# First-stage order of a chunked-attention and two-FFN kernel: products in sub-steps, an early ScalarE table load, and a new table of order

## The chip, the cores and the metric

The kernel runs on one core of one Trainium2 chip. The metric is device time in microseconds (us) of one execution. A core has TensorE (PE in the profile, with PEld for its weight loads), VectorE (DVE), ScalarE (ACT), GpSimd (POOL) and SyncE (SP, which here only starts DMA transfers), each with its own queue of instructions; they meet through semaphores.

## The reference, cut to what matters

```python
# q, k, v: (4, 8, 768, 64); mem_k, mem_v: (4, 8, 8, 64); chunks of 32 queries
for c in range(nc):                       # each chunk sees 8 memory keys + 16 left + 32 own + 8 right
    scores = scale * q_c @ concat(mem_k, k_ctx).T
    a = exp(scores - max(scores)); a = a / (sum(a) + 1e-9)
    out[:, :, c_start:c_end] = a @ concat(mem_v, v_ctx)
x = out.transpose(0, 2, 1, 3).reshape(3072, 512)
h = x @ w_in;  r = max(h, 0);  x = (s * (r * r) + b) @ w_out         # first FFN, 512 -> 2048 -> 512
h = x @ w_in2; x = (max(h, 0) + alpha * min(h, 0)) @ w_out2          # second FFN
```

The four weight matrices arrive as 64-bit floats.

## The kernel before, in words

The 3072 tokens are 24 tiles of 128, and six blocks of four tiles (512 tokens). For each tile the attention makes scores (`sc`), VectorE takes the row maxima (`m`), ScalarE the exponentials (`e`, or `qa` where the tile shares a borrowed buffer), VectorE sums and normalises, TensorE transposes (`pt`, or `turns`), ScalarE copies the result (`aT`), and TensorE multiplies by the values (`px`; `sp` is a bank that takes the scores of one tile and the values of the tile before). Tiles 0 to 3 (`ALONE`) have banks of their own pair; from tile 4 on, one scores-and-values step per tile.

Every factor of a large product is split in a high and a low part of 32 bits, and three products are summed: high by high, high by low, low by high. ScalarE makes the high part of the attention's output (`xh`) and VectorE the low part (`xl`). The weights are handled in 16 parts of 128 hidden columns, `w0` to `w15`, each with an input half and an output half (for `w0` and `w1` the halves, `w0i` and `w0o`, are loaded and converted separately). A conversion takes the raw words through seven passes: ScalarE (`a<-raw`), four on VectorE (L299, L304, L309, L314), ScalarE's high part (L321), VectorE's low part (L327).

A unit is one block and one part f: 12 products into a `ph` bank (function `g1`, L633), an activation in three steps, a split into `gh` and `gl`, and, two units later (`LAG`), 12 products into the four `po` banks (`g2`, L692). The first block's parts 0 to 2 (`HALVES`) are done in two halves of 256 tokens, the left half first. In the first FFN, block 0 goes through its first `SEG` parts, then block 1 through the same ones; both are spilled to DRAM, and each is finished with the remaining parts afterwards. Blocks 2 to 5 then take all 16 parts, and the second FFN follows.

The order of all this is decided when the kernel is built: a class `Plan` holds a list of steps with an engine, a rank and what they wait for, and puts out the steps engine by engine; `Pace` describes TensorE's clock and instruction refills for it. Constants in the class (`RATE`, `FETCH`, and now `AHEAD`) and tables of numbers (`FIRST_LOADS`, the order of the first loads on SyncE's queue; `TILE_RANKS`; `CONV_RANKS`; `STEPS`; `BY_HEAD`, the tiles whose exponentials are taken head by head) set the order in the first stage. What comes out is a fixed sequence for each engine; on the chip each engine runs its own in that order. The ring of `ph` banks has two places, and no more than eight of SyncE's transfers are under way at once.

Of the kernel before, what the change touches and what calls it, by code (L numbers as in the profile page):

```python
# [9 lines left out]
F32 = mybir.dt.float32  # L10
F32R = mybir.dt.float32r
U32 = mybir.dt.uint32
ACTF = mybir.ActivationFunctionType
# [3 lines left out]
P = 128  # L17
# [9 lines left out]
KD, KF = DM // P, DFF // P  # L27
BLK = 512
TPB = BLK // P
# [2 lines left out]
NEG = -1.0e30  # L32
SCALE = 1.0 / float(D) ** 0.5

SEG = 7
LAG = 2
HALVES = 3
PIECES = 2
SPLIT = 2

# [2 lines left out]
SET_SLOTS = {2: 15, 3: 14}  # L43
QA_SLOT = 13

FIRST_LOADS = """q0 q1 w1i v0 q3 w0o q2 v2 w0i v1 w1o q4 v3 w2 w3 w4 v4 w6 q5 v7 q6 v5 q7 w5 w9 v6 w7 w8""".split()

TILE_RANKS = (-280, -85, -170, -175, -15, -240, -5, -260, -85)

BY_HEAD = (1, 2, 4, 5, 6)  # L50

CONV_RANKS = {1: 195, 2: 35, 3: 30, 4: 25, 5: 20, 6: 15, 9: -40, 10: -95, 11: -25, 12: -10, 13: 40, 14: -70}

STEPS = (28, 18, 18, 47, 43, 38)


KHEAD = LEFT + RIGHT
# [25 lines left out]
class Pace:  # L83


    WINDOW, PHASE = 3.41, 2.7
    BLOCK, FIRST = 256, 184

    def __init__(self):
        self.window, self.active, self.warm = 0, 0.0, False  # L90
# [11 lines left out]
    def run(self, t, step, fetch):  # L102

        done, total = 0, max(step.count, 1)
        while done < total:
            at = self.count + done
            block, into = divmod(at - self.FIRST, self.BLOCK)
            if block >= 0 and into == 0:
                t = max(t, self.due[block])
                self.due[block + 1] = t + fetch(t)  # L110
            n = min(total - done, self.BLOCK - into)
            work = step.cost * n / total
            while work > 1e-9:
                self._to(t + 1e-6)
                speed = 1.0 if self.warm else 0.65 if step.dense else 0.53
                left = self.PHASE + (self.window + 1) * self.WINDOW - t
                took = min(left, work / speed)
                self.active += took * (0.5 if step.dense else 1.0)
                work -= took * speed
                t += took  # L120
            done += n
        self.count += total
        return t


class Plan:
# [1 line left out]

    PAST = {"PE": 0.22, "DVE": 0.15, "ACT": 0.2, "POOL": 0.15, "SP": 2.2, "PQ": 2.2}
    NEXT = {"DVE": 0.12, "ACT": 0.12}  # L130
    RATE = 396e3
    LANES = 8
    FETCH = 2.7, 5.3

    def __init__(self, rings):
        self.steps = []
# [10 lines left out]
    def order(self):  # L147
        for s in self.steps:
            s.n_wait = len(s.after)
            for a in s.after:  # L150
                a.outs.append(s)
        engines = {s.engine for s in self.steps}
        open_ = {e: [] for e in engines}
        for s in self.steps:
            if not s.n_wait:
                open_[s.engine].append(s)
        at = {e: 0.0 for e in engines}
        last = {}
        held = {}
        wire = 0.7  # L160
        landed = [0.0] * self.LANES
        pace = Pace()
        due = sorted((s for s in self.steps if s.engine == "SP"), key=lambda s: (-s.rank, -s.seq))
        done = []
        while len(done) < len(self.steps):
            best = None
            for e in engines:
                pick = None
                queue = [due[-1]] if e == "SP" and due else open_[e]
                for s in queue:  # L170
                    if s.n_wait:
                        continue
                    r = s.ready
                    if s.takes:
                        free = self.free[s.takes[0]]
                        if not free:
                            continue
                        r = max(r, min(free.values()))
                    r = max(r, at[e] + (self.NEXT[e] if e in self.NEXT and last.get(e) in s.after else 0.0))
                    if e == "SP" and s.bytes:  # L180
                        r = max(r, landed[-self.LANES])
                    key = (max(r, at[e] + 0.02), s.rank, s.seq)
                    if pick is None or key < pick[0]:
                        pick = (key, r, s)
                if pick and (best is None or pick[1] < best[1]):
                    best = pick
            assert best, [(e, s.rank, s.takes, s.seq) for e in engines for s in open_[e]]
            _, t, s = best
            e = s.engine
            open_[e].remove(s)  # L190
            if e == "SP":
                due.pop()
            slot = None
            if s.takes:
                ring, holder = s.takes
                free = self.free[ring]
                slot = min(free, key=lambda n: (free[n], n))
                del free[slot]
                held[holder] = (ring, slot)
            s.start = t  # L200
            last[e] = s
            at[e] = pace.run(t, s, lambda t: self.FETCH[wire > t + 1.0]) if e == "PE" else t + s.cost
            end = at[e]
            if s.bytes:
                n = max(1, s.bytes >> 18)
                for k in range(n):
                    wire = max(wire, t + s.cost * (k + 1) / n) + s.bytes / n / self.RATE
                    landed.append(wire + self.PAST[e])
                end = wire
            s.end = end + self.PAST[e]  # L210
            for holder in s.frees:
                ring, n = held.pop(holder)
                self.free[ring][n] = s.end
            for o in s.outs:
                o.n_wait -= 1
                o.ready = max(o.ready, at[e] if o.engine == e in ("PE", "DVE", "ACT") else s.end)
                if not o.n_wait:
                    open_[o.engine].append(o)
            done.append((s, slot))
        return done  # L220
# [3 lines left out]
def tile_chunk_attention_two_ffn(ctx: ExitStack, tc: tile.TileContext, qt, kw, vw, win, wout, cst, out):  # L224
    nc = tc.nc
    const = ctx.enter_context(tc.tile_pool(name="const", bufs=1))
# [3 lines left out]
    psum = ctx.enter_context(tc.tile_pool(name="psum", bufs=1, space=bass.MemoryType.PSUM))  # L230
# [4 lines left out]
    xh = [const.tile([P, KD, BLK], F32R, name=f"xh{n}") for n in range(2)]  # L235
    xl = [const.tile([P, KD, BLK], F32R, name=f"xl{n}") for n in range(2)]
# [3 lines left out]
    plan = Plan({"ph": 2, "g": 2, "gg": 3, "ao": 2})  # L240
    slot_of = {}

    def held(holder):
        return slot_of[holder]
# [18 lines left out]


    wts, raws, conv_done, load_done = {}, {}, {}, {}

    def slot_tile(f, mats, shape, dt, name):
        tag = f"w{f}" if len(mats) == 2 else f"w{f}{'io'[mats[0]]}"
# [17 lines left out]
    def convert(layer, f, mats, rank, after):  # L286
        n = len(mats)
# [41 lines left out]
        name = f"w{f}" + ("io"[mats[0]] if n == 1 else "")  # L329
# [7 lines left out]
        hi = plan.add("ACT", 0.02 + 0.51 * n, rank, high, [c4])  # L337
        lo = plan.add("DVE", 0.07 + 0.53 * n, rank, rest, [hi], frees=[key])
        for m in mats:
            conv_done[layer, m, f] = lo  # L340

# [174 lines left out]
    def x_high(i):  # L518
        for pars, px in state[i]["px"]:
            nc.scalar.activation(out=x_of(i, xh, pars), in_=px, func=ACTF.Copy)  # L520
# [35 lines left out]
    def finish_tile(i, r, px):  # L556
        leaves[set_of(i)]["v"] = leaves[set_of(i)]["x"] = px
        more = 0.15 if i in ALONE else 0
        hi = plan.add("ACT", 0.49 + more, r + STEPS[5], lambda: x_high(i), [px] + list(x_users[i // TPB % 2]))
        x_done[i] = plan.add("DVE", 0.61 + more, r + STEPS[5], lambda: x_low(i), [hi])  # L560
        return x_done[i]

# [52 lines left out]
                      [att[t]["aT"] for t in two] + [att[t]["lv"] for t in two], count=256, dense=True)  # L615
        banks_free["pa"] = [finish_tile(t, r3, px) for t in two]

    x_done = {}
    x_users = {0: [], 1: []}


    po = [None] * KD
    ph, gt, gs = {}, {}, {}

    def g1(u):
        layer, j, f, cols = units[u]
        n = (layer * NB + j) % 2
        p = psum.tile([P, BLK], F32, tag=f"ph{held(('ph', u))}", name="ph")[:, :cols.stop - cols.start]
        w = wts[layer, 0, f]
        i = 0  # L630
        for kk in range(KD):
            for a, x in ((1, xh[n]), (0, xl[n]), (0, xh[n])):
                nc.tensor.matmul(p, lhsT=w[:, a, kk * P:(kk + 1) * P], rhs=x[:, kk, cols],  # L633
                                 start=(i == 0), stop=(i == 3 * KD - 1))
                i += 1
        ph[u] = p

    def new_g(u):
        cols = units[u][3]
# [112 lines left out]

    id_ = plan.add("POOL", 0.6, -1000, lambda: make_identity(nc, ident))
    cs = plan.add("ACT", 0.1, -1000, consts)

    for i in range(TPB):
        attention_alone(i, TILE_RANKS[i])
    for i in range(TPB, 2 * TPB + 1):
        r = TILE_RANKS[i]
# [57 lines left out]
    for j in range(2, NB):  # L817
        n_units = (KF - SEG) + 7 if j == 2 else KF
        for i in range(j * TPB, j * TPB + TPB, 2):
            r = when[0, j, 0] - 40 - 10.0 * (TPB - i % TPB) * n_units / TPB  # L820
# [7 lines left out]
    def unit_g1(u):  # L828
        layer, j, f, cols = units[u]
        rank = 10.0 * u  # L830
        n = (layer * NB + j) % 2
        if layer == 0:
            xs = [x_done[j * TPB + t] for t in range(cols.start // P, cols.stop // P)]
        else:
# [3 lines left out]
            xs = [x1_done[j, "x"]]  # L838
        if (layer, j) not in blocks_g1:
# [1 line left out]
            x_users[n] = []  # L841
        width = (cols.stop - cols.start) / BLK
        mm = MM if width == 1 else 0.121
        s = plan.add("PE", 12 * mm, rank, lambda: g1(u), xs + [conv_done[layer, 0, f], id_, in_turn[0]],
                     takes=("ph", ("ph", u)), count=24)
        in_turn[0] = s
        x_users[n].append(s)
        last_user[layer, f, 0] = s
# [156 lines left out]
```

## Time and profile before

| | us |
|---|---|
| median of 3 runs (lowest, highest) | 1143.71 (1139.6, 1144.55) |
| the profiled execution | 1143.53 |
| its span, first to last instruction | 1141.8 |
| TensorE busy | 1114.9 |
| VectorE busy | 605.6 |
| ScalarE busy | 350.8 |
| TensorE busy in the first 60 us | 39.04 |

The span is shorter than the execution by what lies around the instructions. A row of a timeline gives the start, the time busy, the engine, the line, the operation with output and input, the shapes and the count of instructions merged; in brackets stands the idle time before it and what ended it. Products are pipelined, so the time busy of one runs into the next; the distance of two starts is what one costs. The line numbers of the profile before are those of the kernel before; the new kernel's lines lie three to six further on in the parts that are shown.

### The profile page before, as it was taken

What the parts mean: (1) busy time and instruction counts of PE and PEld (TensorE: products, weight loads), DVE (VectorE), ACT (ScalarE), POOL (GpSimd) and SP (SyncE); (2) the same over time, 40 slices, a digit from 0 to 9 for tenths busy, and PEclk for the clock granted to TensorE, in tenths of its full rate; (3) what the DMA queues carried; (4) which work ended last, traced back from release to release, by engine and by line L of the source; (5) the groups of instructions that cost most, each with busy time, mean ns of one, the idle gap of its engine ahead of it and who ended that gap; (6) DMA issues with size and microseconds to landing.
All of it is one profiled execution on the core that took longest, in us unless ns stands there. A gap on an engine that the chain in (4) does not pass through costs nothing.

```text
span 1141.8 us, 18302 instructions
## 1 busy us (share of the span) xinstructions
PE 1114.9 (98%) x7848; PEld 925.2 (81%) x7848; DVE 605.6 (53%) x938; ACT 350.8 (31%) x615; POOL 28.8 (3%) x58
## 2 busy tenths in 40 slices
PE   4799999999999999999999999999999999999998
PEld 4788888888888888888888788888888888888886
DVE  6797935445445355434799744334334434344432
ACT  5675644432232223224564311111111111111111
POOL 0000000000000000000000000000000000000000
PEclk9899999999999999999999999999999999999999
DMA  9918121324112213005557103002002002000000
GB/s 348 345 44 303 59 80 66 130 73 148 38 65 92 83 46 112 1 1 189 180 197 251 69 1 111 1 1 102 10 1 92 19 1 91 21 1 2 37 1 37
DMA packets 46241, 98.32 MB, mean 86 GB/s; under 512 B 4944, under 2 KB 4944, under 8 KB 46160
## 3 DMA queue, kind: packets, MB, share of 16 engines
q1 hardware_dynamic: 40320, 77.22, 19.4%
q0 software_dynamic: 5696, 19.93, 4.5%
q8 instruction: 61, 1.00, 0.4%
q14 instruction: 20, 0.16, 0.1%
q10 hardware_dynamic: 144, 0.01, 0.0%
HBM read 76.16 MB, written 20.97 MB: 85 GB/s over the span
## 4 chain that ended last, share of the span: by engine, by line
PE 52%; issue 42%; DMA 3%; DVE 1%; POOL 1%; ACT 1%; SPq 0%; POOLq 0%; ACTq 0%; DVEq 0%
PE ph L633 25%; PE po L694 23%; PE po L692 3%; DMA raw<-in_wout_dram 2%; POOL x1d L731 1%; DMA kv<-in_kw_dram 1%; DMA raw<-in_win_dram 0%; PE sp L488 0%; DVE a L309 0%; DVE a L314 0%; DMA x1d<-o 0%; PE sp L401 0%; DVE gl L677 0%; PE sc L401 0%; PE turns L466 0%
## 5 line engine op out<-in xcount | busy, mean ns | idle before, releaser
L633 PE MATMUL ph<-xh,w 128*128 128x512 f32 (+1 forms) x1560 | 508.4, 388 | 1.1 <-issue 1.1
L633 PEld LDWEIGHTS ph<-xh,w 128*128 128x128 f32 x1560 | 293.4, 189 | 60.9 <-issue 1.4
L633 PE MATMUL ph<-xl,w 128*128 128x512 f32 (+1 forms) x780 | 301.8, 387 | 0.0
L672 ACT ACTIVATE gh<-g 128x512 fp32r<-128x512 f32 (+1 forms) x195 | 121.8, 625 | 462.9 <-DVE g L664 380.4
L692 PE MATMUL po<-gh,w 128*128 128x512 f32 (+1 forms) x792 | 257.5, 387 | 0.1
L694 PE MATMUL po<-w,gh 128*128 128x512 f32 x768 | 251.6, 389 | 1.0 <-DVE o L728 1.0
L677 DVE TENSOR_TENSOR gl<-g,gh 128x512 fp32r<-128x512 f32 (+1 forms) x195 | 133.0, 682 | 106.5 <-ACT gh L672 106.0
L659 DVE TENSOR_SCALAR g<-ph,cst_sb 128x512 f32<-128x512 f32 x96 | 72.0, 750 | 206.6 <-PE ph L633 206.5
L692 PEld LDWEIGHTS po<-gh,w 128*128 128x128 f32 x792 | 148.6, 189 | 30.3 <-DVE o L728 0.7
L633 PEld LDWEIGHTS ph<-xl,w 128*128 128x128 f32 x780 | 147.5, 189 | 29.1
L694 PEld LDWEIGHTS po<-w,gh 128*128 128x128 f32 x768 | 144.1, 188 | 31.6 <-DVE o L728 1.8
L692 PE MATMUL po<-gl,w 128*128 128x512 f32 (+1 forms) x396 | 152.0, 384 | 0.0
L694 PE MATMUL po<-w,gl 128*128 128x512 f32 x384 | 149.4, 389 | 0.0
L644 ACT ACTIVATE g<-ph 128x512 f32<-128x512 f32 (+1 forms) x99 | 57.9, 585 | 156.4 <-PE ph L633 155.1
L651 DVE TENSOR_TENSOR g<-g 128x512 f32<-128x512 f32 x48 | 33.2, 692 | 111.6 <-ACT g L644 111.6
L692 PEld LDWEIGHTS po<-gl,w 128*128 128x128 f32 x396 | 74.9, 189 | 14.2
L694 PEld LDWEIGHTS po<-w,gl 128*128 128x128 f32 x384 | 72.1, 188 | 15.0
L655 DVE TENSOR_SCALAR g<-g,cst_sb 128x512 f32<-128x512 f32 (+1 forms) x99 | 52.9, 534 | 45.1 <-ACT g L649 43.5
L664 DVE SCALAR_TENSOR_TENSOR g<-ph,g 128x512 f32<-128x512 f32 x96 | 66.3, 691 | 3.1
L321 ACT ACTIVATE w<-a 128x1024 fp32r<-128x1024 f32 (+1 forms) x36 | 34.8, 967 | 34.8 <-DVE a L314 33.6
L296 ACT ACTIVATE a<-raw 128x1024 f32<-128x1024 f32 (+1 forms) x36 | 37.6, 1044 | 22.2 <-DVE w L327 13.7
L327 DVE TENSOR_TENSOR w<-a,w 128x1024 fp32r<-128x1024 f32 (+1 forms) x36 | 39.5, 1100 | 3.0 <-ACT w L321 3.0
(81 smaller groups left out, 506.2 us busy)
## 6 DMA issues: line engine op xcount, KB each, us to landing
raw<-in_win_dram SPq DMA_DIRECT2D x64, 256.0 KB, 4.8
raw<-in_wout_dram SPq DMA_DIRECT2D x64, 256.0 KB, 5.2
x1d<-o POOLq DMA_DIRECT2D x24, 512.0 KB, 3.6
vd<-in_vw_dram SPq DMA_DIRECT2D x40, 256.0 KB, 5.6
kd<-in_kw_dram SPq DMA_DIRECT2D x20, 368.0 KB, 4.9
xh<-x1d SPq DMA_DIRECT2D x6, 1024.0 KB, 5.6
xl<-x1d SPq DMA_DIRECT2D x6, 1024.0 KB, 7.7
qT<-in_qt_dram SPq DMA_DIRECT2D x20, 256.0 KB, 4.2
```

The costliest lines, as they stand in the source:

```text
L296: nc.scalar.activation(out=temp["a"], in_=words(1).bitcast(F32), func=ACTF.Abs)
L321: nc.scalar.activation(out=w[:, :, 0, :], in_=temp["a"], func=ACTF.Copy)
L327: nc.vector.tensor_sub(out=w[:, :, 1, :], in0=temp["a"], in1=w[:, :, 0, :].bitcast(F32))
L633: nc.tensor.matmul(p, lhsT=w[:, a, kk * P:(kk + 1) * P], rhs=x[:, kk, cols], start=(i == 0), stop=(i == 3 * KD - 1))
L644: nc.scalar.activation(out=new_g(u), in_=ph.pop(u), func=ACTF.Relu)
L655: nc.vector.tensor_scalar(out=g, in0=g, scalar1=cst_sb[:, 0:1], scalar2=cst_sb[:, 1:2], op0=ALU.mult, op1=ALU.add)
L659: nc.vector.tensor_scalar(out=new_g(u), in0=ph[u], scalar1=0.0, scalar2=cst_sb[:, 2 + f:3 + f], op0=ALU.min, op1=ALU.mult)
L664: nc.vector.scalar_tensor_tensor(out=g, in0=ph.pop(u), scalar=0.0, in1=g, op0=ALU.max, op1=ALU.add)
L672: nc.scalar.activation(out=gh, in_=gt[u], func=ACTF.Copy)
L677: nc.vector.tensor_sub(out=gl, in0=gt.pop(u), in1=gh.bitcast(F32))
L692: nc.tensor.matmul(po[d][:, cols], lhsT=w[:, a, ds_], rhs=g, start=start, stop=stop)
L694: nc.tensor.matmul(po[d], lhsT=g[:, ds_], rhs=w[:, a, :], start=start, stop=stop)
```

## The change

The `ph` products of block 0 and 1 in the parts below `APART` = 6 are planned as three steps of four instead of one of twelve: high by high as soon as the high parts of tokens and weights are there, then the four with the tokens' low part and the four with the weights' low part (for part 0 the other way round). A one-column exponential on ScalarE, with a memset on VectorE for its input, stands at the very start, so that ScalarE's table of functions is loaded there. The tables of order are new, `SEG` goes from 7 to 9, `BY_HEAD` has tile 3 in place of tile 6, and the constants by which the plan reckons are changed.

```diff
-SEG = 7
+SEG = 9
+APART = 6
-FIRST_LOADS = """q0 q1 w1i v0 q3 w0o q2 v2 w0i v1 w1o q4 v3 w2 w3 w4 v4 w6 q5 v7 q6 v5 q7 w5 w9 v6 w7 w8""".split()
-TILE_RANKS = (-280, -85, -170, -175, -15, -240, -5, -260, -85)
-BY_HEAD = (1, 2, 4, 5, 6)
+FIRST_LOADS = """q0 q1 w1i v0 q3 w0i q2 v1 w0o v2 w1o q4 w2 v3 w3 w7 w4 w6 v7 q6 q5 v5 v4 w5 w8 w9 v6 q7""".split()
+TILE_RANKS = (-60, -235, -190, -540, -10, -390, -20, -440, -125)
+BY_HEAD = (1, 2, 3, 4, 5)
...
-    BLOCK, FIRST = 256, 184
+    BLOCK, FIRST, AHEAD = 256, 184, 48
...
-    RATE = 396e3
+    RATE = 382e3
-    FETCH = 2.7, 5.3
+    FETCH = 1.6, 5.1
...
+    def first_exp():
+        nc.scalar.activation(out=zero, in_=zero, func=ACTF.Exp)
+    zd = plan.add("DVE", 0.1, -1000, lambda: nc.vector.memset(zero, 0.0))
+    plan.add("ACT", 1.7, -999, first_exp, [zd])
...
-        s = plan.add("PE", 12 * mm, rank, lambda: g1(u), xs + [conv_done[layer, 0, f], id_, in_turn[0]],
-                     takes=("ph", ("ph", u)), count=24)
+        if layer == 0 and j < 2 and f < APART:
+            his = [x_hi[j * TPB + t] for t in range(cols.start // P, cols.stop // P)]
+            s = plan.add("PE", 4 * mm, rank, lambda: g1(u, ((0, 0),), True, False), his + [conv_high[f], id_, in_turn[0]],
+                         takes=("ph", ("ph", u)), count=8)
+            rest = [(((1, 0),), [conv_done[layer, 0, f]]), (((0, 1),), xs)]
+            for n_, (kinds, needs) in enumerate(rest if f == 0 else rest[::-1]):
+                s = plan.add("PE", 4 * mm, rank, lambda kinds=kinds, n_=n_: g1(u, kinds, False, n_ == 1), [s, *needs], count=8)
+        else:
+            s = plan.add("PE", 12 * mm, rank, lambda: g1(u, ((1, 0), (0, 1), (0, 0))), xs + [conv_done[layer, 0, f], id_, in_turn[0]],
+                         takes=("ph", ("ph", u)), count=24)
```

The order on ScalarE at its start, before:

```order
L751 DMA cst_sb<-in_cst_dram 128x18
L296 ACT_TABLE_LOAD
L296 ACTIVATE a<-raw 128x512
L433 ACTIVATE e<-e 128x512
L452 ACTIVATE e,rs<-sc,nm 128x64 x6
L296 ACTIVATE a<-raw 128x512
L471 ACTIVATE aT<-pt 128x512
L452 ACTIVATE e,rs<-sc,nm 128x64 x2
```

and after:

```order
L755 DMA cst_sb<-in_cst_dram 128x18
L763 ACT_TABLE_LOAD
L763 ACTIVATE zero<-zero 128x1
L438 ACTIVATE e<-e 128x512
L299 ACTIVATE a<-raw 128x512
L457 ACTIVATE e,rs<-sc,nm 128x64 x8
```

The table load has moved ahead of the first conversion's pass, tile 0's exponential (`e<-e`) ahead of it too, and tile 1's eight exponentials by head stand in one run.

TensorE at its start (`sc`, `sp<-kd` are scores, `px` values, `pt` transposes, `ph` and `po` the products of the units; 32 instructions are one tile), before:

```order
L401 MATMUL sc<-kd,qT 32x64 x64
L466 MATMUL pt<-ident,e 128x128 x4
L488 MATMUL px<-aT,vd 64x32 x32
L466 MATMUL pt<-ident,e 128x128 x4
L401 MATMUL sc<-kv,qa 32x64 x32
L488 MATMUL px<-aT,vd 64x32 x32
L401 MATMUL sp<-kd,qT 32x64 x32
L401 MATMUL sc<-kv,qa 32x64 x32
L633 MATMUL ph<-xh_74,w 128x256
L633 MATMUL ph<-xl_76,w 128x256
```

and after:

```order
L406 MATMUL sc<-kd,qT 32x64 x64
L471 MATMUL pt<-ident,e 128x128 x8
L493 MATMUL px<-aT,vd 64x32 x64
L639 MATMUL ph<-xh_74,w 128x256 x4
L406 MATMUL sc<-kv,qa 32x64 x64
L406 MATMUL sp<-kd,qT 32x64 x32
L639 MATMUL ph<-xh_74,w 128x256 x4
L639 MATMUL ph<-xl_76,w 128x256 x4
L639 MATMUL ph<-xh_74,w 128x256 x4
L639 MATMUL ph<-xl_76,w 128x256 x4
L639 MATMUL ph<-xh_74,w 128x256 x4
L471 MATMUL pt<-ident,qa 128x128 x4
```

Four `ph` products stand ahead of the scores of tiles 3, 2 and 4, the scores of all three now come in one run, and the transposes of tiles 0 and 1 and their values stand together.

TensorE around the last of the eight first tiles, where only values are left in the `sp` step, before:

```order
L692 MATMUL po_793<-gh,w 128x256
L692 MATMUL po_793<-gl,w 128x256
L692 MATMUL po_793<-gh,w 128x256
L466 MATMUL turns<-ident,qa 128x128 x4
L488 MATMUL sp<-qa,kv 64x32 x32
L692 MATMUL po_751<-gh,w 128x512
```

and after:

```order
L471 MATMUL turns<-ident,qa 128x128 x4
L696 MATMUL po_723<-gh,w 128x512
L696 MATMUL po_723<-gl,w 128x512
L696 MATMUL po_723<-gh,w 128x512
L696 MATMUL po_730<-gh,w 128x512
L696 MATMUL po_730<-gl,w 128x512
L696 MATMUL po_730<-gh,w 128x512
L493 MATMUL sp<-qa,kv 64x32 x32
```

Six `po` products now stand between the transposes and the values that wait for their copy.

More of the change, by code (lines that the diff above doesn't have):

```diff
@@ L44 @@
 QA_SLOT = 13
-FIRST_LOADS = """q0 q1 w1i v0 q3 w0o q2 v2 w0i v1 w1o q4 v3 w2 w3 w4 v4 w6 q5 v7 q6 v5 q7 w5 w9 v6 w7 w8""".split()
-TILE_RANKS = (-280, -85, -170, -175, -15, -240, -5, -260, -85)
-BY_HEAD = (1, 2, 4, 5, 6)
-CONV_RANKS = {1: 195, 2: 35, 3: 30, 4: 25, 5: 20, 6: 15, 9: -40, 10: -95, 11: -25, 12: -10, 13: 40, 14: -70}
-STEPS = (28, 18, 18, 47, 43, 38)
+FIRST_LOADS = """q0 q1 w1i v0 q3 w0i q2 v1 w0o v2 w1o q4 w2 v3 w3 w7 w4 w6 v7 q6 q5 v5 v4 w5 w8 w9 v6 q7""".split()
+TILE_RANKS = (-60, -235, -190, -540, -10, -390, -20, -440, -125)
+BY_HEAD = (1, 2, 3, 4, 5)
+CONV_RANKS = {2: -50, 3: 10, 4: 20, 5: -55, 6: 5, 7: 40, 8: 30, 9: -5, 10: -40, 12: 50, 13: 20, 14: -90, 15: 75}
+STEPS = (51, 70, 47, 120, 94, 71)
 KHEAD = LEFT + RIGHT
@@ L109, in run @@
                 t = max(t, self.due[block])
+            if block >= 0 and into == self.AHEAD:
                 self.due[block + 1] = t + fetch(t)
-            n = min(total - done, self.BLOCK - into)
+            n = min(total - done, self.AHEAD - into if into < self.AHEAD else self.BLOCK - into)
             work = step.cost * n / total
@@ L206, in order @@
                 for k in range(n):
-                    wire = max(wire, t + s.cost * (k + 1) / n) + s.bytes / n / self.RATE
+                    wire = max(wire, t + s.cost * (k + 1) / n) + s.bytes / n / self.RATE + (1.2 if len(landed) == self.LANES + 2 else 0.0)
                     landed.append(wire + self.PAST[e])
@@ L265, in tile_chunk_attention_two_ffn @@
     wts, raws, conv_done, load_done = {}, {}, {}, {}
+    conv_high = {}
     def slot_tile(f, mats, shape, dt, name):
@@ L340, in convert @@
             conv_done[layer, m, f] = lo
+        if layer == 0 and 0 in mats:
+            conv_high[f] = hi
     sets = {}
@@ L558, in finish_tile @@
         more = 0.15 if i in ALONE else 0
-        hi = plan.add("ACT", 0.49 + more, r + STEPS[5], lambda: x_high(i), [px] + list(x_users[i // TPB % 2]))
+        hi = x_hi[i] = plan.add("ACT", 0.49 + more, r + STEPS[5], lambda: x_high(i), [px] + list(x_users[i // TPB % 2]))
         x_done[i] = plan.add("DVE", 0.61 + more, r + STEPS[5], lambda: x_low(i), [hi])
@@ L616, in attention_of_two @@
         banks_free["pa"] = [finish_tile(t, r3, px) for t in two]
-    x_done = {}
+    x_done, x_hi = {}, {}
     x_users = {0: [], 1: []}
@@ L623, in tile_chunk_attention_two_ffn, with g1 @@
     ph, gt, gs = {}, {}, {}
-    def g1(u):
+    def g1(u, kinds, first=True, last=True):
         layer, j, f, cols = units[u]
         n = (layer * NB + j) % 2
-        p = psum.tile([P, BLK], F32, tag=f"ph{held(('ph', u))}", name="ph")[:, :cols.stop - cols.start]
+        if first:
+            ph[u] = psum.tile([P, BLK], F32, tag=f"ph{held(('ph', u))}", name="ph")[:, :cols.stop - cols.start]
         w = wts[layer, 0, f]
[L630 to L636, printed above, removed]
+        each = [(kk, a, (xh, xl)[b][n]) for kk in range(KD) for a, b in kinds]
+        for i, (kk, a, x) in enumerate(each):
+            nc.tensor.matmul(ph[u], lhsT=w[:, a, kk * P:(kk + 1) * P], rhs=x[:, kk, cols],
+                             start=first and i == 0, stop=last and i == len(each) - 1)
     def new_g(u):
@@ L754, in tile_chunk_attention_two_ffn @@
     cs = plan.add("ACT", 0.1, -1000, consts)
+    zero = const.tile([P, 1], F32, name="zero")
+    def first_exp():
+        nc.scalar.activation(out=zero, in_=zero, func=ACTF.Exp)
+    zd = plan.add("DVE", 0.1, -1000, lambda: nc.vector.memset(zero, 0.0))
+    plan.add("ACT", 1.7, -999, first_exp, [zd])
     for i in range(TPB):
```

## Prediction

> **What bounds the kernel now.** I read the page first, then TensorE's busy time in two windows, its waits up to 100 us, and the timelines of TensorE, ScalarE and VectorE up to 90 us. From the page, the span and the line of busy shares:
>
> ```profile
> span 1141.8 us, 18302 instructions
> PE 1114.9 (98%) x7848; PEld 925.2 (81%) x7848; DVE 605.6 (53%) x938; ACT 350.8 (31%) x615; POOL 28.8 (3%) x58
> ```
>
> The sum below is made against this execution's own 1143.53 us, 0.18 under the median of the three runs (1143.71); 0.5% of it, about what a measurement here can tell from no change, is 5.7 us. The windows (time, TensorE busy, granted clock, DMA share, GB/s) say where the 2% lie:
>
> ```profile
> 0.00:60.00 60.00, 39.04 (x973) 0.91 0.97 348
> 60.00:1138.00 1078.00, 1075.88 (x6877) 1.00 0.20 71
> ```
>
> After 60 us TensorE is idle for 2.1 us in all, at full clock; before that for 21, part of it at half clock. The change moves work only there. The waits of TensorE up to 100 us ("issue" is time in which nothing in the profile held it):
>
> ```profile
> PE sc L401 <- DMA kd<-in_kw_dram: 6.1, 2, 4.7
> PE sp L488 <- issue: 2.5, 1, 2.5
> PE sp L401 <- issue: 2.0, 1, 2.0
> PE sp L401 <- ACT xh L520: 1.8, 1, 1.8
> PE ph L633 <- issue: 1.1, 1, 1.1
> PE px L488 <- issue: 0.4, 1, 0.4
> ```
>
> TensorE's timeline, with the steps used below and one row of the chain of waits for twelve 512-wide products:
>
> ```profile
> 13.40 1.09 PE L466 MATMUL pt<-ident,e 128*128 128x128 f32 x4 [4.97 <-DVE e L475]
> 15.17 1.93 PE L488 MATMUL px<-aT,vd 64*64 64x32 f32 x64 [0.69 <-ACT aT L471]
> 17.80 1.08 PE L466 MATMUL pt<-ident,e 128*128 128x128 f32 x4 [0.70 <-ACT xh L520]
> 26.72 0.58 PE L633 MATMUL ph<-xh,w 128*128 128x256 f32 x1
> 33.56 0.66 PE L466 MATMUL pt<-ident,qa 128*128 128x128 f32 x4 [0.16 <-DVE qa L475]
> 36.19 0.53 PE L488 MATMUL px<-qa,kv 64*64 64x32 f32 x18 [0.38 <-issue]
> 43.49 0.85 PE L488 MATMUL sp<-aT,vd 64*64 64x32 f32 x19 [2.54 <-issue]
> 44.26 0.58 PE L692 MATMUL po<-gh,w 128*128 128x256 f32 x1
> 44.85 0.41 PE L692 MATMUL po<-gh,w 128*128 128x256 f32 x1
> 45.07 0.41 PE L633 MATMUL ph<-xh,w 128*128 128x256 f32 x1
> 50.75 0.28 PE L692 MATMUL po<-gh,w 128*128 128x256 f32 x1
> 50.87 0.28 PE L692 MATMUL po<-gl,w 128*128 128x256 f32 x1
> 57.03 0.86 PE L401 MATMUL sp<-kv,qa 64*32 64x64 f32 x64
> 57.81 1.14 PE L488 MATMUL sp<-aT,vd 64*64 64x32 f32 x64
> 58.88 0.39 PE L692 MATMUL po<-gh,w 128*128 128x256 f32 x1
> 83.61 1.13 PE L488 MATMUL sp<-qa,kv 64*64 64x32 f32 x64 [0.72 <-ACT qa L471]
> ...
> 656.27 2.72 PE po L694 x12
> ```
>
> From the first po product at 44.26 on TensorE no longer waits, but for 0.72 us at 83.61. It restarts there at half clock (256-wide products begin 0.22 apart; at full clock 0.12). So I forecast one milestone, the first po product, and what is done ahead of it. ScalarE's opening:
>
> ```profile
> 8.72 1.28 ACT L296 ACT_TABLE_LOAD   x1 [8.72 <-DMA raw<-in_win_dram]
> 10.02 0.66 ACT L296 ACTIVATE a<-raw 128x512 f32<-128x512 f32 x1
> 10.58 0.61 ACT L433 ACTIVATE e<-e 128x512 f32<-128x512 f32 x1
> 12.38 0.30 ACT L452 ACTIVATE e<-sc,nm 128x64 f32<-128x64 f32 x1
> ```
>
> VectorE: one row of its timeline, five groups by form up to 45 us, and its waits up to 60 us:
>
> ```profile
> 7.00 0.75 DVE L429 TENSOR_TENSOR e<-sc,m 128x256 f32<-128x256 f32 x2
> L309 DVE SCALAR_TENSOR_TENSOR a<-raw,a 128x512 uint32<-128x512 uint32 x4 | 2.8, 688 | 0.1
> L475 DVE TENSOR_TENSOR e<-e,rs 128x512 f32<-128x512 f32 x3 | 2.0, 683 | 0.0
> L299 DVE TENSOR_SCALAR a<-a 128x512 f32<-128x512 f32 x4 | 1.7, 423 | 1.5 <-ACT a L296 1.5
> L299 DVE TENSOR_SCALAR a<-a 128x1024 f32<-128x1024 f32 x2 | 1.4, 686 | 0.0
> L309 DVE SCALAR_TENSOR_TENSOR a<-raw,a 128x1024 uint32<-128x1024 uint32 x1 | 1.2, 1218 | 0.0
> DVE sp L418 <- PE sp L488: 3.9, 1, 3.9
> DVE a L299 <- ACT a L296: 1.5, 1, 1.5
> ```
>
> From about 10 to 40 us VectorE hardly waits: it is what the opening is made of. Its long waits are 1.5 us ahead of the first conversion and 3.9 us behind the stall that ends at 43.49.
>
> **The change, part by part.** *Table.* The load (1.28) stands behind a weight's arrival at 8.72, and tile 0's exp, ready at 7.75, starts at 10.58. Loaded at once, exp starts at 7.8. The added memset and one-column exp run while both engines have nothing else. Worth 2.8 us to tile 0's exp; what VectorE puts next eats part of it.
>
> *Opening order.* VectorE now does tile 1's maxima and three pieces of w1's conversion ahead of tile 0's normalised e: 8.4 + sums 0.6 + maxima 0.7 + pieces and small ones 1.7 + e 0.7 = 12.1, against 13.25. Tile 1's eight exps run unbroken from 10.25 (8 x 0.30, 12.8), so its e ends at 13.9 and its transposes start at 14.0 instead of 17.80. Two values steps of 1.93 (15.1 to 19.0) and ScalarE's copy (0.7) give the first ph product at 19.7 instead of 26.72: 7 us earlier. This is the part that looks large.
>
> *Three sub-steps.* The twelve products of a unit remain twelve; only waits are added, in a place where TensorE is idle anyway, so I cost them at nothing. Behind a waiting sub-step stand the next transposes, and those wait for VectorE.
>
> *Loads.* SyncE's queue now puts v4 behind eight weights. Ahead of its end lie 15.5 MB, by the window's 348 GB/s 45 us; TensorE asks for it at about 51. Hidden, with 4 to 6 us to spare.
>
> *Where the 7 us go.* The scores of tiles 3, 2 and 4 now stand behind the first ph products and need bank space that tile 1's low part frees at 21.3 (19.7, a conversion pass, and its own 0.7 with a little waiting). Then VectorE has, up to the normalised e of tiles 3 and 2, by the order: six 512-wide conversion passes (four of 0.69, of which I count 0.6, as passes overlap by about 0.08, and two of 0.42: 3.2), two 1024-wide ones of 0.6 and two of 1.14, three maxima of about the same 0.65, small ones 1.0, two e 1.2: 10.8 us, with 0.6 of waits for ScalarE 11.4, so 32.7. Before, the last transposes of these tiles ran at 33.56. Transposes and unit 2's products (four groups of 0.9 at half clock) reach 35.8; the two values steps 1.07 to 1.93 each, 38 to 39.6; then ScalarE's copy 0.65 and VectorE's low part 0.7. First po product: 39.5 without a stall.
>
> *The stall.* Two attention steps back to back were held by "issue" 2.5 us at 43.49, and 0.4 at 36.19. The two values steps now stand back to back as well. Bounds 0 and 2.5, and a half-clock or full-clock values step besides; I take 2, nearer to the larger, as the DMA share of the first 60 us is 0.97: milestone 41.5 (39.5 to 43). The Trainium skill, Runtime: NRT & Kernel Launch, section Instruction fetch mechanics, says that the sequencer refills its instructions in blocks of 256 over its own DMA queue and that this is mostly hidden. The trace does not agree for this stage: four "issue" waits make 6.0 us. By that rule the milestone would be 39.5 and the time 1139.1.
>
> *Bookkeeping.* At the milestone the new order has done unit 2's twelve products (12 x 0.12 = 1.44) more, and one scores-and-values step (0.78 + 1.07 = 1.85, rows at 57.03 to 58.88) less. So 44.26 - 41.5 - 1.85 + 1.44 = 2.35 us gained. Both restart at half clock.
>
> *Nine parts instead of seven ahead of block 1.* From 41.5 to the unit of w7 TensorE has 108 products of 0.12 and 2.1 for the slow start, seven times 2.72, three steps of 1.85 and three transposes of 0.4: 41 us, to 82.5. VectorE has in that stretch four whole conversions (4.6 each), parts of two (3.5), tiles 4 to 7 (8.7) and units 2 to 9 (7.3): 38 us, with some 3 of waits 82.5. They arrive together; before, with two conversions less, VectorE had room. I charge 0.7 us of waits. The 0.72 at 83.61 goes, since six po products now stand between the transposes and the values step.
>
> Sum: 2.35 + 0.72 - 0.7 = 2.4 us; 1143.5 - 2.4 = 1141.1.
>
> **Rivals.** *Faster by over 0.5%.* The values steps run without a stall (39.5) and TensorE is already at full clock, which saves 22 x 0.10 = 2.2. That is 2.4 + 2 + 2.2 = 6.6, less up to 1 that w7 then holds: 1137.2 to 1138. For it: the 0.4 wait of 36.19. Against: VectorE is even with TensorE at 82.5, so what comes earlier is waited for later. The Trainium skill, TensorE: Matmul & The Clock Gate, Part 1, says that full clock comes after about 3.4 us of sustained work, in a window that runs free of the kernel; by it the values steps could have TensorE at full clock by the milestone. The trace agrees in size: half clock still at 45.07, full at 50.75.
>
> *Nothing left.* VectorE needs 2 to 3 us more than my sum to w5, w6 or w7; TensorE waits that long: 1143.5 (1142.5 to 1146). For it: no slack in the sum; against: pieces that overlap more than I allow.
>
> *Slower.* Each weight part costs VectorE 2 x 0.69 + 3 x 1.22 = 5.0 us and a unit's own two passes 1.1, against TensorE's 5.44 a unit (two of 2.72). With six whole units in a row ahead of block 1, each can lose 0.7 and tiles 5 to 7 add 8; if they fall in front of w7 and w8, both units wait. It decides from a lag of 8.1 us (5.7 + 2.4) at w7's low part: about 1151. Against: that low part stands behind tile 7's maxima only.
>
> **How the numbers follow.** Forecast 0.52 (1139 to 1143), faster rival 0.20, nothing left 0.20, slower 0.08. Faster by over 0.5% (under 1138.0) 0.20, within 0.72, slower (over 1149.4) 0.08. The range, 1136.5 to 1146.5, takes in the faster rival and nothing left.
>
> **What would show it.** Right: the table load ahead of 3 us, tile 0's exp near 7.8, the first ph product near 20, VectorE without long waits from 8 to 35, the first po product at 40 to 43, a wait of TensorE on VectorE's w near 80, none behind the last transposes. Wrong: first po product before 39 or after 44, no "issue" wait in the opening, or TensorE waits of several us between 60 and 95.

## The result, and the profile after

| | us |
|---|---|
| kernel after, median of 4 runs (lowest, highest) | 1155.66 (1155.37, 1156.19) |
| kernel before on the same chip, median | 1144.13 |
| ratio after to before, 95% interval | 1.011 (1.0083 to 1.0136) |
| profiled execution of after | 1155.69 |
| its span | 1153.9 |

The changed kernel is 11.5 us slower, where 2.4 us faster was forecast, and it lies outside the range. In experiment 8 and in the kernel before with the early load alone, one run each was far slower at a lower granted clock (1642.78 us at 0.641, 1247.7 us at 0.852); it counts in the median given there, but not in the ratio. First the page's line of busy shares, then TensorE's windows (time, TensorE busy, weight loads, VectorE, ScalarE, GpSimd, granted clock, DMA share, GB/s), both of the kernel after:

```profile
PE 1133.8 (98%) x7848; PEld 926.8 (80%) x7848; DVE 606.6 (53%) x938; ACT 349.5 (30%) x616; POOL 28.9 (3%) x58
```

```profile
0.00:60.00 60.00, 44.53 (x880) 40.66 (x880) 48.11 (x102) 40.78 (x134) 0.69 (x6) 0.91 0.90 332
60.00:1150.00 1090.00, 1089.26 (x6970) 886.10 (x6968) 558.53 (x837) 308.15 (x483) 28.25 (x52) 1.00 0.20 71
```

TensorE has the same 7848 instructions and is busy 18.9 us longer (1114.9 before). It idles less than before, in the first 60 us (15.5 us against 21) and after them (0.7 against 2.1), and the granted clock is 0.91 and 1.00 as before. So the time went into neither a wait nor a lower clock. All waits of TensorE in the whole run of after:

```profile
PE sc L406 <- DMA kd<-in_kw_dram: 6.0, 2, 4.6
PE pt L471 <- DVE e L480: 3.8, 1, 3.8
PE pt L471 <- DVE qa L480: 2.8, 1, 2.8
PE ph L639 <- issue: 0.9, 1, 0.9
PE pt L471 <- ACT a L299: 0.8, 1, 0.8
PE sc L406 <- issue: 0.7, 1, 0.7
PE ph L639 <- ACT xh L525: 0.5, 1, 0.5
PE turns L471 <- DVE e L480: 0.4, 1, 0.4
PE po L698 <- DVE o L732: 0.2, 1, 0.2
```

The opening even went a little better than forecast. ScalarE's rows, then TensorE's, of the timeline of after:

```profile
1.18 1.28 ACT L763 ACT_TABLE_LOAD   x1 [1.18 <-PEq L1010]
7.70 0.63 ACT L438 ACTIVATE e<-e 128x512 f32<-128x512 f32 x1 [5.02 <-DVE e L434]
```

```profile
12.14 1.09 PE L471 MATMUL pt<-ident,e 128*128 128x128 f32 x4 [3.77 <-DVE e L480]
14.00 1.09 PE L471 MATMUL pt<-ident,e 128*128 128x128 f32 x4 [0.77 <-ACT a L299]
19.15 1.22 PE L639 MATMUL ph<-xh,w 128*128 128x256 f32 x4 [0.50 <-ACT xh L525]
31.56 0.63 PE L471 MATMUL pt<-ident,qa 128*128 128x128 f32 x4 [2.82 <-DVE qa L480]
34.13 3.73 PE L493 MATMUL px<-qa,kv 64*64 64x32 f32 x128
38.81 0.41 PE L696 MATMUL po<-gh,w 128*128 128x256 f32 x1
39.02 0.41 PE L696 MATMUL po<-gl,w 128*128 128x256 f32 x1
```

What is left is the price of a product. The chain of waits far behind the opening, at 690 us (start, us, what), of before and then of after:

```profile
691.63 2.72 PE ph L633 x12
694.35 2.72 PE po L694 x12
```

```profile
695.17 2.80 PE ph L639 x12
697.97 2.75 PE po L698 x12
```

Twelve `ph` products cost 2.80 us in place of 2.72, 0.2333 us each in place of 0.2267, at the same shape, clock and order. The groups of the page say it for the whole run, before and after. Behind the first bar stand the time in which the group was busy (us) and the mean duration of one product (ns); it is the mean that counts here, 388 and 387 ns before, 395 and 394 after, since the busy time of a group also depends on which products overlap:

```profile
L633 PE MATMUL ph<-xh,w 128*128 128x512 f32 (+1 forms) x1560 | 508.4, 388 | 1.1 <-issue 1.1
L633 PE MATMUL ph<-xl,w 128*128 128x512 f32 (+1 forms) x780 | 301.8, 387 | 0.0
```

```profile
L639 PE MATMUL ph<-xh,w 128*128 128x512 f32 (+1 forms) x1560 | 511.9, 395 | 0.5 <-ACT xh L525 0.5
L639 PE MATMUL ph<-xl,w 128*128 128x512 f32 (+1 forms) x780 | 299.7, 394 | 0.9 <-issue 0.9
```

There are 192 units of 2 x 12 products in the kernel (two FFNs, six blocks, 16 parts): 0.08 us on each unit's `ph` half alone make 15.4 us.

### The profile page after: what moved, and what is told of

The parts are those of the page before. It is cut to its first block, busy times and chain, and to the rows that moved or that the text cites. A ratio compares the mean times of both kernels' runs of the same rounds, so it can differ in the third digit from the quotient of the medians.

```text
span 1153.9 us, 18310 instructions
## 1 busy us (share of the span) xinstructions
PE 1133.8 (98%) x7848; PEld 926.8 (80%) x7848; DVE 606.6 (53%) x938; ACT 349.5 (30%) x616; POOL 28.9 (3%) x58
## 4 chain that ended last, share of the span: by engine, by line
PE 54%; issue 40%; DMA 2%; DVE 2%; ACT 1%; POOL 1%; SPq 0%; POOLq 0%; ACTq 0%; DVEq 0%
PE ph L639 26%; PE po L698 23%; PE po L696 4%; POOL x1d L735 1%; DMA raw<-in_wout_dram 1%; DMA x1d<-o 1%; PE px L493 0%; DMA qT<-in_qt_dram 0%; ACT qa L457 0%; DMA kd<-in_kw_dram 0%; PE sp L493 0%; PE sc L406 0%; DVE a L312 0%; ACT e L457 0%; DVE a L317 0%
```

## The experiments

**What could make a product dearer.** The `ph` product's code hardly changed, and from the second FFN on not at all. What did change everywhere is where things lie in SBUF, the memory on the core, in which every tile has a start address in bytes that is the same in all 128 partitions. The one-column tile `zero` stands in the same pool as the tokens `xh` and `xl`, behind them. The built program gives it 32 bytes per partition, and all that follows, the weights and the hidden activations `gh` and `gl`, lies 32 bytes further on: weights at 49920 in place of 49888, tokens at 17120 as before. A product reads a slice of such tiles, and all slices lie whole multiples of 512 bytes from the start of the first tile, so a shift is the same for every product of a kind. Theory A: what counts is the distance of a product's two operands in SBUF (`ph`: tokens and weights; `po`: hidden activations and weights, which moved together). Theory B: the new order or the sub-steps make the products dearer.

Twelve runs, in three sets of four on one chip each. The times of before beside them were 1142.81, 1143.0 and 1142.97 us (medians of 22, 23 and 29 runs).

**1. The tile moved to the last pool**, with the order of TensorE's instructions as after:

```diff
-    zero = const.tile([P, 1], F32, name="zero")
+    zero = small.tile([P, 1], F32, tag="zero", bufs=1, name="zero")
```

> The changed kernel with its one-column tile taken from the last pool instead of the first, so that weights and the buffers of the units lie 32 bytes lower, where they lay before the change; order and instructions stay. Theory A (the tile pushed the weights by 32 bytes against the tokens, and each ph product costs 0.233 us instead of 0.227): ph units back at 2.72 us, some 2304 x 0.0066 = 15 us less than the changed kernel, 1138 to 1141, under the kernel before. Theory B (the new order or the sub-steps slow the ph products): 1155 as the changed kernel, ph units 2.80.

Measured: 1138.37 us, ratio 0.9965 (0.995 to 0.9979). The chain at 690 us:

```profile
692.57 2.72 PE ph L639 x12
695.29 2.72 PE po L698 x12
```

The place of four bytes takes away 17.3 us (1155.66 to 1138.37), and what is left of the change is faster than before by 4.4. TensorE is busy 1114.8 us, as in the kernel before (1114.9). Theory B fell.

**2. The kernel before with an unused tile behind the tokens:**

```diff
     xl = [const.tile([P, KD, BLK], F32R, name=f"xl{n}") for n in range(2)]
+    pad = const.tile([P, 1], F32, name="pad")
...
+    plan.add("DVE", 0.1, -1000, lambda: nc.vector.memset(pad, 0.0))
```

> The kernel before with an unused one-column tile between the tokens' and the weights' tiles (and one memset for it), nothing else. Theory A: ph units at 2.80 us and 1144 + 15 = 1159 (1157 to 1161). Theory B: 1144, ph units 2.72.

Measured: 1159.56 us, ratio 1.0148 (1.0123 to 1.0173). The loss comes with the tile and its memset alone, without any other part of the change, 16.8 us over 1142.81:

```profile
692.60 2.75 PE po L695 x12
695.35 2.80 PE ph L634 x12
```

**3. The tile ahead of the tokens**, so that tokens and weights both move 32 bytes and their distance is that of before:

```diff
+    zero = const.tile([P, 1], F32, name="zero")
     xh = [const.tile([P, KD, BLK], F32R, name=f"xh{n}") for n in range(2)]
```

> The changed kernel with the one-column tile ahead of the tokens' tiles: tokens and weights both move by 32 bytes against the kernel before, their distance is that of before. Theory A with distance as what counts: 1138 to 1141, ph units 2.72. Theory A with the weights' own place as what counts (they lie as in the changed kernel): 1155, ph units 2.80. Theory B: 1155.

Measured: 1137.65 us, ratio 0.9956 (0.9941 to 0.9971), the lowest time of all, though its interval overlaps that of experiment 1. The weights lie at 49920 as in after, so it isn't their own address:

```profile
691.74 2.72 PE ph L640 x12
694.46 2.72 PE po L699 x12
```

**4 to 7. The size of the tile**, and with it the shift of the weights against the tokens:

```diff
-    zero = const.tile([P, 1], F32, name="zero")
+    zero = const.tile([P, 16], F32, name="zero")[:, 0:1]      # and 24, 32, 64
```

64 bytes:

> The changed kernel with the one-column tile grown to 64 bytes: the weights lie 64 bytes higher than before, that is 64 more against the tokens. Theory A with a pattern that repeats every 64 bytes: 1138 to 1141, ph units 2.72. With one that repeats every 128 bytes or more: 1150 to 1160, ph units over 2.75. Theory B: 1155.

96 bytes:

> The kernel after, with 96 bytes for the added tile. If the distance counts by a period of 128, this is 32 short of a whole one: slow as at 32 and 64 is 2.80 us per twelve products and 1154 to 1157; if only half of each period is slow, 2.72 and 1137 to 1139. A value between (2.76, some 1146) would say that the cost grows with the distance from a whole period.

128 bytes:

> The kernel after, with 128 bytes per partition (32 numbers) for the added tile in place of 4, so that the weights lie 128 bytes further from the tokens than in the kernel before. Only distance counts, with a period of 128 bytes: units of ph back at 2.72 us per twelve products, time 1137 to 1139. Period 256 bytes or more (po's operands, which ran at 2.72, lie 256 apart by 512): 2.80 and 1154 to 1157. If any tile behind the tokens in the same pool slowed the products, whatever its size: 1154 to 1157 as well.

256 bytes:

> The kernel after, with 256 bytes for the added tile. Shifts of 32 to 128 bytes were all slow. If the distance counts by a period of 256 bytes (the operands of po lie 256 from a whole 512 and ran at 2.72): ph 2.72 and 1137 to 1139. If the period is 512 or more: ph 2.79 to 2.81 and 1152 to 1156.

Twelve `ph` products and time, with the distance of tokens and weights worked out from the addresses:

| shift, bytes | distance, bytes | twelve `ph`, us | time, us | ratio to before (interval) |
|---|---|---|---|---|
| 0 (experiment 1) | 32768 | 2.72 | 1138.37 | 0.9965 (0.995 to 0.9979) |
| 32 (after) | 32800 | 2.80 | 1155.66 | 1.011 (1.0083 to 1.0136) |
| 64 | 32832 | 2.80 | 1154.79 | 1.0108 (1.0086 to 1.0131) |
| 96 | 32864 | 2.81 | 1154.72 | 1.0116 (1.0096 to 1.0137) |
| 128 | 32896 | 2.79 | 1152.78 | 1.0098 (1.0078 to 1.0117) |
| 256 | 33024 | 2.72 | 1138.6 | 0.9971 (0.9957 to 0.9984) |

The rows of 128 and of 256 bytes:

```profile
694.67 2.79 PE ph L639 x12
```

```profile
697.66 2.72 PE ph L639 x12
```

A period of 64 bytes and one of 128 fell; a shift of 256 bytes brings the old price back. The distances that ran fast, 32768 and 33024, are whole multiples of 256. That fits a period of 256 but doesn't prove one: shifts from 160 to 224 and beyond 256 weren't tried.

**8. The hidden activations moved alone.** The tile at the head of their pool: tokens and weights as before, `gh` and `gl` 32 bytes further from both.

```diff
-    zero = const.tile([P, 1], F32, name="zero")
+    zero = work.tile([P, 1], F32, tag="zero", name="zero")
```

> The kernel after, with the added tile at the head of the pool that holds the hidden activations g: tokens and weights in their places of before, gh and gl 32 bytes further from both. If the rule is on the two operands of a product: ph stays at 2.72 us per twelve products (distance as before); po, whose operands now lie 32 further apart, goes to 2.80 if its old distance was a favoured one as well (1153 to 1156), or stays at 2.72 (1137 to 1140) if 256 apart is nothing special. If instead what counts is the tokens that TensorE reads against the g that ScalarE and VectorE write at the same time: ph at 2.80, po at 2.72, and 1153 to 1156.

Measured: 1155.32 us, ratio 1.0122 (1.0099 to 1.0145). The dear half has changed sides:

```profile
690.71 2.73 PE ph L639 x12
693.45 2.79 PE po L698 x12
```

So the same holds for `po`, whose distance was 165632, also a multiple of 256, and here 165664. That the tokens read by TensorE meet the writes of ScalarE and VectorE to `g` fell: that distance changed here too, and `ph` stayed at 2.73.

**9 to 12. What the rest of the change is worth**, all with the weights in their place of before. Sub-steps out (`APART = 0`):

> The kernel after with the added tile in the last pool (weights in their place of before), and without the three sub-steps: all units are one step of twelve products; tables of order as after, so the plan comes out anew. The version with sub-steps took 1138.4. If the sub-steps carry the gain: the first po product 3 to 5 us later and 1141 to 1143. If order and table load carry it: 1138 to 1139. Against that stands that the tables were found for sub-steps; a unit that waits for its last operand holds what stands behind it: up to 1146.

Tables of order, `BY_HEAD` and `SEG` of before, with sub-steps, early load and the plan's new constants:

> The version with the weights in their place of before (1138.4), with the tables of order and SEG of the kernel before; sub-steps, early table load and the plan's constants as after. The early load alone, in the kernel before, gave nothing (1143.0), and the version without sub-steps kept all but 0.6 us. If the gain is the new order's: 1142 to 1145. If sub-steps and table load bring it with any order: 1138 to 1140.

Early table load out (its two `plan.add` lines):

> The version with the weights in their place of before (1138.4), without the one-column exponential and its memset; all else as after. If the early load only helps together with the new order, which lets tile 0's exponential stand ahead of the conversion: 1 to 3 us lost, 1139.5 to 1141.5. If the order alone does it (the load then comes with tile 0's exponential, at 7.8 us, where ScalarE has little else): 0 to 1.3 us lost, 1138 to 1139.7.

The kernel before with the early table load alone:

> The kernel before, with nothing but the one-column exponential and its memset at the start, the tile for it in the last pool (weights in their place). If the early table load is worth what it takes off tile 0's exponential (2.8 us) down to the first po product: 1140 to 1141.5 beside 1142.8 to 1144. If VectorE's work, unchanged, sets the opening: 0 to 1 us, 1142 to 1144.

| | time, us | ratio to before (interval) |
|---|---|---|
| all but the shift (experiment 1) | 1138.37 | 0.9965 (0.995 to 0.9979) |
| without sub-steps | 1139.02 | 0.9971 (0.9958 to 0.9984) |
| without early load | 1139.01 | 0.9977 (0.9962 to 0.9992) |
| with the old tables | 1140.98 | 0.999 (0.9975 to 1.0005) |
| before with early load alone | 1143.02 | 1.0 (0.998 to 1.002) |

The new order seems to carry the larger part: with the old tables 2.6 us are lost against experiment 1 (1138.37 to 1140.98), though the two intervals still overlap a little, and 2.0 us of the gain stay (1142.97 to 1140.98), which the interval doesn't tell from none. Taking out the sub-steps or the early load costs 0.6 us each, less than the intervals can tell. No run has the new tables alone. The early load alone gives nothing: ScalarE's exponential of tile 0 came 1.4 us earlier than in the kernel before (10.58), but the first `po` product, 44.26 before, moved 0.24:

```profile
9.17 0.61 ACT L433 ACTIVATE e<-e 128x512 f32<-128x512 f32 x1
44.02 0.58 PE L692 MATMUL po<-gh,w 128*128 128x256 f32 x1
```

In experiment 1 the saving can be counted. The first `po` product and the clock behind it, and then TensorE's waits from 60 to 100 us:

```profile
40.49 0.42 PE L696 MATMUL po<-gh,w 128*128 128x256 f32 x1
41.77 1.12 PE L639 MATMUL ph<-xh,w 128*128 128x256 f32 x8
```

```profile
PE turns L471 <- ACT g L648: 0.6, 1, 0.6
PE sp L493 <- issue: 0.4, 1, 0.4
```

44.26 - 40.49, less 0.41 of bookkeeping as in the prediction, makes 3.4. Six products follow at half clock where before it was some 22: 16 x 0.095 = 1.5. The 0.72 at 83.61 is gone, and 1.0 of small waits is new. Sum 4.6, by the spans 4.5 (1141.8 to 1137.3). Waits beyond 100 us, 1.0 before and 0.6 here, would make it 5.0, so the working is good to about half a us.

## Why the prediction was wrong

**The step that failed** is in the first part: "The change moves work only there", the first 60 us. With it went the row of 2.72 us for twelve products, taken for both kernels alike. The edit that broke it I costed as two instructions that run "while both engines have nothing else". That is right for the instructions, but they bring a tile, and a tile takes a place: 4 bytes, 32 in the pool, 0.08 us on 192 units. No term of the sum and no rival had the price of a product in it, so the range couldn't hold the time. My slower rival (VectorE late at w7, 0.08) is not what happened: after the opening TensorE waited for VectorE 0.4 us, at 60.74, and 0.2 at 635.46.

By the 512-wide groups the shift costs 6 ns on each of 2268 `ph` products (396 against 390 in experiment 1), 13.6 us, and 0 to 2 ns on as many `po`, up to 4.5; between the spans of after and experiment 1 lie 16.6. `po` rises a little too when only `ph` is shifted (2.72 to 2.75), and the trace of after shows where: between 620 and 1120 us the first five `po` products behind each `ph` unit begin on average 228 to 236 ns apart, the other seven 227. Why the slowness outlasts the `ph` products stays open.

The Trainium skill, SBUF — State Buffer, section A bandwidth-pool intuition that's wrong, gives TensorE a second, independent read port for loading weights beside that of the moving operand, which by itself would leave no room for one operand's place to slow the other's stream. The runs do not agree as far as that goes: 2.72 or 2.80 us by nothing but the distance of the two (experiments 1 and 3 against after).

The trace of experiment 8 narrows down which two reads meet. A product holds one operand in place (the stationary one, loaded by a PEld instruction of its own while the product before still runs: in the kernel before, the load for the product at 1137.32 starts at 1137.10, together with the product ahead of it) and streams the other (the moving one). At the end of a `ph` unit the moving operand is the tokens, and the load that runs beside the last product is that of the first `po` product. In the first FFN `po`'s stationary operand is a weight, at a multiple of 256 from the tokens, and the first `po` product begins 227 ns after the last `ph` product (mean of 54 pairs); in the second FFN it is `gh`, 32 bytes off, and it takes 235 ns (mean of 88 pairs). The `ph` product's own two operands lie alike in both. So the pair that counts there is the moving operand of the running product and the stationary operand of the next, not the two operands of one product; inside a unit both have the same remainder, so the other experiments can't tell them apart. That it is the two reads which disturb each other is still inferred: no run takes one of them away.

**Point by point, the steps that concern the opening:**

- Table: load ahead of 3 us (1.18), tile 0's exponential at 7.70, forecast 7.8. Right. That it is "worth 2.8 us to tile 0's exp" is right, that so little comes through to the end is what the single experiments show.
- Opening order: transposes of tiles 0 and 1 at 12.14 and 14.00 (forecast 12.1 and 14.0), first `ph` product at 19.15 (19.7). Right.
- Sub-steps: costed at nothing; without them 0.6 us more, which can't be told from nothing. Right as far as the runs tell.
- Loads: TensorE didn't wait for v4 in after. In the profiles of experiments 7 and 8 it did, 0.7 and 1.1 us at about 50 us, so there were not 4 to 6 us to spare. (The list has seven weights ahead of v4, two of them in halves, not eight; the 15.5 MB are right for these.)
- VectorE's stretch: last tiles' transposes from 31.56 (32.7). About right.
- The stall: I took 2 us at the two values steps. They ran through in one piece at 34.13, half clock, 3.73 us. Mis-sized: the first `po` product came at 38.81 (41.5 with the stall, 39.5 without), outside the 39.5 to 43 I gave. The "issue" waits were 0.9 and 0.7 in place of 6.0. The step that failed here is that two values steps back to back bring the stall. Counted over TensorE's products and weight loads in order, the four "issue" waits of before stand at numbers 706, 962, 1219 and 1474, those of after at 706 and 963: they lie 256 instructions apart, to within one, whatever runs there. In after the next such place lies inside the two values steps, at 36.99, without a wait, and the one after that, where before lost 2.5 us just ahead of its milestone, lies behind the milestone, at 49.49, without a wait either. The length varies: with the same order on TensorE, the profile of experiment 7 (256 bytes) waited 0.7 at the place inside the values steps. The Trainium skill, Runtime: NRT & Kernel Launch, section Instruction fetch mechanics, by which the refill of instructions is mostly hidden, was nearer here than the trace of before; with 1.6 us left it is not wholly so.
- Clock: half clock at the milestone as forecast (38.81 to 39.02 is 0.21). It is not fixed, though: in experiment 8, same order on TensorE, the values steps took 2.64 us and `po` products began 0.13 apart at 39.02. That is what the faster rival asked for; in experiment 7 the clock was full there too (products at 40.00 and 40.12), in after and in experiments 1 and 3 half. In after TensorE ran without a wait from 31.56, and the granted clock was still 0.50 from 33 to 43 us: ten us of unbroken work hadn't brought the full clock back.

```profile
35.87 2.64 PE L493 MATMUL px<-qa,kv 64*64 64x32 f32 x128
39.02 0.28 PE L696 MATMUL po<-gh,w 128*128 128x256 f32 x1
39.15 0.28 PE L696 MATMUL po<-gl,w 128*128 128x256 f32 x1
```

- Nine parts ahead of block 1: the 0.7 us of waits on w5 to w7 didn't come, in experiment 1 neither, where products cost what they did before; so VectorE was not the limit at 82.5. Wrong by that 0.7.
- The 0.72 at 83.61 went. Right. The reading that TensorE waits nowhere else behind 44.26 missed 0.47 at 631.37 and 0.49 at 636.26, of which 0.23 was left in after.

Without the shift the change brought 4.4 us (experiment 1) or 5.2 (experiment 3) in place of 2.4. The 2 us of the stall would account for the first; in the profile of experiment 1 it came another way, since the milestone was 40.49 and the clock rose sooner. So the opening gained about twice what the sum had, in the direction that was forecast.

## What to carry to other kernels

Ask of every added or resized tile what it pushes: list the addresses of a product's two operands in both builds, and compare their distances, before any time is forecast. When a kernel gets slower with the same instructions, full clock and fewer waits, compare the time of one repeated group far from the edit; it says at once whether the loss is a stage's or a product's. Put small tiles into the last pool, where they move nothing, or pad them to a size that keeps the distance (256 bytes did it here).

## What the hardware showed that I had not expected

A 512-wide product of 32-bit operands cost 0.2267 us where the two operands lay a multiple of 256 bytes apart in SBUF (32768, 33024, 165632), and 0.2325 to 0.2342 us where they were 32, 64, 96 or 128 bytes off (2.79 to 2.81 for twelve). As far as experiment 8 tells, the two that count are the moving operand of the running product and the stationary operand that is loaded beside it for the next. It is the distance, not the place of either, and it holds for tokens against weights and for hidden activations against weights. Over the kernel that is 14 to 17 us, three to four times what the whole reordering brought.

TensorE's "issue" waits in the opening came 256 instructions apart (706, 962, 1219, 1474 in the kernel before), with 0.4 to 2.5 us each; after 60 us the same places brought none in before and after, and 0.4 us once in experiment 1. What decides whether such a place brings a wait isn't shown.
